# Spectral stage on Trainium2: transposed tiles hold neighbouring frequencies in pairs, with the input's and the tokens' order changed to suit

## Chip, cores and metric

One core of a Trainium2 chip runs the whole program: a spectral layer, a mixture of experts with top-1 routing and a feed-forward layer with maxima. The metric is the device time of one execution in microseconds. Matrix products that need accuracy are written as sums of a rounded part and a rest (`...h` and `...l`), so one product is three matmuls; matmuls of plain float32 operands appear as two instructions each.

## What is computed

```python
X = np.fft.rfft(x, axis=1)                     # x: 8 x 3072 x 256
Yr = Xr @ w_r - Xi @ w_i + b_r
Yi = Xr @ w_i + Xi @ w_r + b_i
Yr = np.sign(Yr) * np.maximum(np.abs(Yr) - 0.01, 0)     # Yi alike
y = np.fft.irfft(Yr + 1j * Yi, n=3072, axis=1)
x = y.reshape(8 * 3072, 256)
skip = (x @ w_skip) <= 0                       # such tokens pass through
e = argmax(x @ w_gate); x += gate * (relu(x @ w1[e]) @ w2[e])
h = np.maximum(np.maximum(x @ v1, x @ v2), x @ v3)
out = h @ w_out
```

## The kernel before

Three functions run one after the other: `spectral`, `experts`, `feed_forward`. Only `spectral` is changed. It treats the 8 batches in turn, and a transform of 3072 = 96 x 32 points is done in two steps of matmuls with a transposition of 32 x 32 blocks on VectorE between them.

*Forward.* `f1_mm` (L264) multiplies a chunk of the input, 96 partitions by 32 times 16 columns, by a 96-point transform; the result lies in a PSUM bank. `f1_tr` (L268) transposes the bank on VectorE into `g2`, a tile of 128 partitions, 32 frequencies and 256 channels; 24 of the 32 are used (`NF`), and the memory of the other eight, `spare(g2)`, later holds `y1s`. Sixteen groups `g` make up a batch. `f2` (L281) takes 128 channels of one frequency of `g2` as the weights (the stationary operand) and the matrix `c2` of that frequency as the moving one.

*Middle.* In a loop over 12 pairs of frequencies, `i`, TensorE runs `f2(i)`, then `wmm(i-1)` (the complex product with the weights, L316), then `if2(i-2)` (the first inverse step, L345). ScalarE and VectorE round and subtract between them (L132, L135, L288, L323 to L328), and ScalarE evicts the result of `if2` into two tiles `zs`, one for each half of the channels (L347).

*Inverse.* `z_tr` (L352) transposes a whole `zs` of 4096 elements per partition into `zt`. `if1` (L357) takes single frequencies of `zt` as weights, four of them in a bank, and ScalarE evicts the bank with a rearrangement (L358) into `y0` (first half) or `y1` (second half). `to_rows` (L364, L365) turns 128 tokens back into rows and adds the gate's scores; ScalarE puts them into `yk` (L366), and the SP queue stores 256 columns of them to DRAM (L367), 24 blocks of 128 tokens per batch. `gating` and `dispatch` (L461) later send the rows to their experts.

The schedule is the order of the code, on every engine. Behind the loop over `i` of a batch that has a successor stand: groups 0 to 3 of the next batch's `f1` (within the last turn), `f1` of groups 4 to 9, `z_tr` of the first half, `if1` for eight groups of it, `z_tr` of the second half, `f1_tr` of groups 4 to 9, `f1` and `f1_tr` of groups 10 to 15, and then for each of eight groups `if1` of the second half and `to_rows` of the group before. Since `y1s` is memory of the next `g2`, the first of those evictions waits until the last `f1_tr` is done. Meanwhile VectorE decodes weights of the feed-forward stage (`decode`, L475 to L527), up to two units per batch; it reads pairs of 32-bit words as `lo, hi = w[:, :, 0], w[:, :, 1]`, so at a step of two words. The last batch has no `f1` to do, and runs `gating` in pieces between the groups. PSUM tags A to D have two banks each, the inputs `xc` four buffers, and `z` tiles three.

Of the kernel before, what the change touches and what calls it, by code (L numbers as in the profile page):

```python
# [21 lines left out]
NF = 24  # L22
# [15 lines left out]
def _constants():  # L38
# [59 lines left out]
    tok = 32 * (32 * r[None] + p // 4) + 4 * g[None] + p % 4  # L98
# [69 lines left out]
def spectral(tc, ins, rows, xo, wsc, base, small, ident, split, feed, G):  # L168
    nc = tc.nc
    x = ins["x"]  # L170
    with ExitStack() as ctx, ExitStack() as early:
# [31 lines left out]
        def load_x(b, chunks):  # L203
            t = []
            for c in chunks:
                a = xp.tile([N1, N2, 32], F32, tag="x", name="xc")
                nc.sync.dma_start(out=a, in_=x[b, c])
                t.append(a)
            return t

        with tc.manual_schedule():
# [49 lines left out]
            def f1_mm(b, xt, g, tag):  # L261
                p = bank(tag, (N2, 16))
                c, o = divmod(g * 16, 32)
                nc.tensor.matmul(p, lhsT=f1, rhs=xt[c][:, :, o:o + 16])  # L264
                return p

            def f1_tr(g2, g, p):
                nc.vector.transpose(  # L268
                    out=g2[:, :, 16 * g:16 * g + 16].rearrange("p s d -> p d s"),
                    in_=p.rearrange("p n d -> p d n"),  # L270
                )

            def spare(g2):
                return g2[:, NF:32].rearrange("p s d -> p (s d)")

            def f2(g2, i, meanwhile=None):
                p = bank("B", (4, 128))
                for j in range(2):
                    f = 2 * i + j
                    for k in range(2):  # L280
                        nc.tensor.matmul(  # L281
                            p[:, 2 * j + k], lhsT=g2[:, f, 128 * k:128 * k + 128], rhs=c2[:, f]
                        )
# [53 lines left out]
            def if2(zs, i, y):  # L337
                p = bank("D", (2, 256))
                for j in range(2):
                    f = 2 * i + j  # L340
                    if i == NP - 1:
                        nc.tensor.matmul(p[:, j], lhsT=ic2[:, j], rhs=y[:, j])
                        continue
                    for n, (a, w) in enumerate(((ic2h, y[0]), (ic2l, y[0]), (ic2h, y[1]))):
                        nc.tensor.matmul(p[:, j], lhsT=a[:, f], rhs=w[:, j], start=(n == 0), stop=(n == 2))  # L345
                for h in range(2):
                    nc.scalar.activation(  # L347
                        out=zs[h][:, 2 * i:2 * i + 2], in_=p[:, :, 128 * h:128 * h + 128], func=AF.Copy
                    )

            def z_tr(zs, zt):
                nc.vector.transpose(out=zt.rearrange("p n e -> p e n"), in_=zs.rearrange("p f e -> p e f"))  # L352

            def if1(zt, dst, g):
                p = bank("D", (4, N1))
                for j in range(4):
                    nc.tensor.matmul(p[:, j], lhsT=zt[:, 4 * g + j], rhs=ic1)  # L357
                nc.scalar.activation(out=dst.rearrange("p (m n) -> p n m", n=4), in_=p, func=AF.Copy)  # L358

            def to_rows(b, g, y0, y1):  # L360
                for r in range(3):
                    t = 3 * g + r
                    p = bank("ABC"[r], (CW,))
                    nc.tensor.matmul(p[:, 0:CW // 2], lhsT=y0[:, 128 * r:128 * r + 128], rhs=gi[:, 0:CW // 2])  # L364
                    nc.tensor.matmul(p[:, CW // 2:CW], lhsT=y1[:, 128 * r:128 * r + 128], rhs=gi[:, CW // 2:CW])  # L365
# [3 lines left out]
                            "(m n) d -> m n d", n=N2  # L369
                        )[:, 4 * g:4 * g + 4],  # L370
# [178 lines left out]
            def new_g2():  # L549
                return ec.tile([128, 32, 256], F32, tag="g2", name="g2")  # L550
# [39 lines left out]
            for b in range(B):  # L590
# [11 lines left out]
                zs = [zp.tile([128, 32, 128], F32, tag="z", name=f"zs{h}") for h in range(2)]  # L602
                for t in zs:
                    nc.gpsimd.memset(t[:, NF:32], 0.0)
# [48 lines left out]
                def trans(h):  # L653
                    zt = zp.tile([128, 32, 128], F32, tag="z", name=f"zt{h}")
# [536 lines left out]
def _layout(name, a):  # L1191
    if name == "x":
        a = a.reshape(B, N1, N2, 8, 32).transpose(0, 3, 1, 2, 4)
# [32 lines left out]
```

## Time and profile before

| | |
|---|---|
| median of 3 runs | 3028.78 us (3018.82 to 3028.97) |
| the profiled execution | 3028.35 us, its span 3026.6 us |
| mean granted clock of TensorE | 0.979 |
| TensorE matmul / weight loads busy | 2891.4 us (96%) / 2502.2 us (83%) |
| VectorE / ScalarE / GpSimd busy | 1919.2 (63%) / 1407.6 (47%) / 1222.3 us (40%) |

PE is TensorE, PEld its weight loads (which overlap matmuls), DVE VectorE, ACT ScalarE, POOL GpSimd, SP the engine that issues most transfers. In the timelines a row is a group of like instructions that follow each other: start in us, time from the first start to the last end, what it is, and in brackets the idle time of the engine before it and what ended that. In the groups by line stand the number of instructions, their busy time in us and the mean in ns, then the idle time before them. In the stretches stand the length in us, the busy time and count of PE, PEld, DVE, ACT and POOL, then the granted clock, the transfers' share of 16 engines, and GB/s. A busy share says little of one stage: the spectral stage, up to some 893 us of the span, is read by itself.

### The profile page before, as it was taken

How to read it: one execution, taken by the hardware profiler on the slowest of the kernel's cores; microseconds unless marked ns; L12 is line 12 of the kernel's file. 1: busy time of each engine (PE TensorE's matmuls, PEld its weight loads, DVE VectorE, ACT ScalarE, POOL GpSimd, SP SyncE). 2: the span in 40 equal slices, each digit the busy share in tenths (PEclk: the TensorE clock that was granted, in tenths of full speed). 3: DMA queues.
4: the chain of work that ended last, by engine and by line, in shares of the span. 5: the costliest groups of instructions: out<-in, count | busy, mean ns of one | idle time of the engine just before them, and what ended most of it. 6: DMA issues, size and time to landing. Idle time of an engine off the chain costs nothing.

```text
span 3026.6 us, 53435 instructions
## 1 busy us (share of the span) xinstructions
PE 2891.4 (96%) x17158; PEld 2502.2 (83%) x17159; DVE 1919.2 (63%) x2707; ACT 1407.6 (47%) x2657; POOL 1222.3 (40%) x1206
## 2 busy tenths in 40 slices
PE   9989889999969999999789999999999999999998
PEld 7779878977959999999767777777777777777776
DVE  7887888778654544545365666666666666666664
ACT  4435544544532333333245555545555555545553
POOL 2032132223242222223245556555555556555554
PEclk9999999999979999999989999999999999999999
DMA  5323332331133333333355665566555665566543
GB/s 151 122 65 111 110 95 78 110 118 50 68 137 107 94 101 100 92 101 101 87 151 161 176 176 161 162 169 180 164 162 162 176 176 161 162 169 180 164 148 112
DMA packets 402461, 398.84 MB, mean 132 GB/s; under 512 B 274962, under 2 KB 320614, under 8 KB 402292
## 3 DMA queue, kind: packets, MB, share of 16 engines
q1 hardware_dynamic: 387732, 369.81, 43.3%
q0 software_dynamic: 14560, 26.86, 2.5%
q8 instruction: 97, 1.59, 0.2%
q14 instruction: 72, 0.59, 0.1%
HBM read 307.69 MB, written 101.91 MB: 135 GB/s over the span
## 4 chain that ended last, share of the span: by engine, by line
PE 45%; DVE 3%; ACT 1%; issue 1%; DMA 0%; SPq 0%; POOL 0%; DVEq 0%
PE pa L1040 18%; PE o_ps L1118 12%; PE pb L1040 10%; PE pc L1040 4%; DVE m L1086 1%; ACT hh L1097 1%; DVE xl L999 1%; DVE m L1050 0%; ACT xh L996 0%; DVE xc L978 0%; DMA xs<-xt 0%; SPq L972 0%; POOL hl L1098 0%; DVE xt L983 0%; DVE t L1050 0%
## 5 line engine op out<-in xcount | busy, mean ns | idle before, releaser
L1040 PE MATMUL pa<-xh,wu 128*128 128x512 f32 x1728 | 616.8, 397 | 19.5 <-ACT xh L996 19.2
L1047 ACT ACTIVATE s<-pa 128x512 f32<-128x512 f32 x648 | 378.6, 595 | 339.4 <-PE pa L1040 216.4
L1098 POOL TENSOR_TENSOR hl<-m,hh 128x512 fp32r<-128x512 f32 x288 | 398.0, 1403 | 301.4 <-ACT hh L1097 301.4
L1040 PEld LDWEIGHTS pa<-xh,wu 128*128 128x128 f32 x1728 | 326.1, 189 | 99.7 <-ACT xh L996 19.4
L1040 PE MATMUL pb<-xh,wu 128*128 128x512 f32 x864 | 348.3, 403 | 7.4 <-DVE m L1050 5.9
L1040 PE MATMUL pa<-xl,wu 128*128 128x512 f32 x864 | 343.2, 397 | 3.7 <-DVE xl L999 3.7
L1118 PE MATMUL o_ps<-hh,wo 128*128 128x512 f32 x1152 | 340.7, 398 | 3.4 <-ACT hh L1097 3.4
L1077 POOL TENSOR_TENSOR t<-s,s 128x512 f32<-128x512 f32 x144 | 186.5, 1295 | 268.4 <-ACT s L1047 268.4
L1118 PEld LDWEIGHTS o_ps<-hh,wo 128*128 128x128 f32 x1152 | 217.4, 189 | 57.1 <-ACT hh L1097 4.7
L907 ACT ACTIVATE hh<-h_ps 128x512 fp32r<-128x512 f32 x208 | 119.7, 597 | 298.1 <-PE h_ps L902 288.2
L1047 ACT ACTIVATE s<-pb 128x512 f32<-128x512 f32 x216 | 129.3, 599 | 272.3 <-PE pb L1040 272.0
L1086 DVE TENSOR_TENSOR m<-m,t 128x1536 f32<-128x1536 f32 x144 | 251.7, 1748 | 0.0
L908 DVE SCALAR_TENSOR_TENSOR hl<-h_ps,hh 128x512 fp32r<-128x512 f32 x208 | 138.7, 689 | 175.9 <-ACT hh L907 158.3
L925 PE MATMUL y_ps<-w2l,hh 128*128 128x256 f32 x832 | 236.1, 284 | 0.6 <-POOL w2l L770 0.2
L925 PE MATMUL y_ps<-w2h,hl 128*128 128x256 f32 x832 | 235.7, 283 | 0.1
L925 PE MATMUL y_ps<-w2h,hh 128*128 128x256 f32 x832 | 235.3, 283 | 0.0
L461 POOL DMA_INDIRECT rows<-yk,pos x192 | 195.2, 1017 | 92.8 <-issue 64.1
L902 PE MATMUL h_ps<-xh,w1h 128*128 128x256 f32 x832 | 230.1, 277 | 1.6 <-DVEq L884 1.6
L902 PE MATMUL h_ps<-xl,w1h 128*128 128x256 f32 x832 | 230.1, 277 | 0.0
L902 PE MATMUL h_ps<-xh,w1l 128*128 128x256 f32 x832 | 229.8, 276 | 0.0
L1040 PEld LDWEIGHTS pb<-xh,wu 128*128 128x128 f32 x864 | 163.1, 189 | 65.1 <-DVE m L1050 15.9
L1050 DVE TENSOR_TENSOR t<-pc,s 128x512 f32<-128x512 f32 x144 | 99.3, 689 | 167.3 <-PE pc L1040 137.1
(248 smaller groups left out, 7212.7 us busy)
## 6 DMA issues: line engine op xcount, KB each, us to landing
wu<-wsc SPq DMA_DIRECT2D x216, 896.0 KB
xc<-in_x_dram SPq DMA_DIRECT2D x64, 384.0 KB
xt<-yk SPq DMA_DIRECT2D x192, 128.0 KB
xs<-xt SPq DMA_DIRECT2D x192, 128.0 KB
out_dram<-ob SPq DMA_DIRECT2D x192, 128.0 KB
xr<-rows SPq DMA_DIRECT2D x53, 264.0 KB
xs<-rows SPq DMA_DIRECT2D x208, 64.0 KB, 2.3
w1f<-in_moe_w_dram SPq DMA_DIRECT2D x9, 1024.0 KB, 4.9
```

The source lines that it names most:

```text
L461: a = nc.gpsimd.indirect_dma_start(out=rows[:, :], out_offset=bass.IndirectOffsetOnAxis(ap=pos, axis=0), in_=yk[:, t, G:G + RW], in_offset ...
L902: nc.tensor.matmul(p[:, j], lhsT=a[:, k, f0:f0 + 128], rhs=v[:, k], start=(i == 0), stop=(i == 5))
L907: nc.scalar.activation(out=hh[:, sl], in_=p, func=AF.Relu)
L908: nc.vector.scalar_tensor_tensor(out=hl[:, sl], in0=p, scalar=0.0, in1=hh[:, sl].bitcast(F32), op0=ALU.max, op1=ALU.subtract)
L925: nc.tensor.matmul(y, lhsT=a[:, c, 128 * j:128 * j + 128], rhs=v[:, c], start=(i == 0), stop=(i == 23))
L1040: nc.tensor.matmul(o, lhsT=self.w[:, g, at:at + 128], rhs=v[h], start=(start and i == 0), stop=(i == 2), skip_group_check=True,)
L1047: nc.scalar.activation(out=self.s[k], in_=o, func=AF.Copy)
L1050: nc.vector.tensor_tensor(out=self.t[:, i], in0=o, in1=self.s[k], op=ALU.add)
L1077: nc.gpsimd.tensor_tensor(out=self.t[:, 2], in0=self.s[5], in1=self.s[7], op=ALU.add)
L1086: nc.vector.tensor_tensor(out=m[:, 0:3], in0=m[:, 0:3], in1=self.t, op=ALU.max)
L1098: nc.gpsimd.tensor_tensor(out=hl[:, i], in0=m[:, i], in1=hh[:, i].bitcast(F32), op=ALU.subtract)
L1118: nc.tensor.matmul(o, lhsT=wo[g][:, 2 * p + c, 128 * k:128 * k + 128], rhs=h[v][:, (0, 3, 1, 2)[2 * t + c]], start=(p == 0 and i == 0), st ...
```

## The change

The two tiles that VectorE's transposes write or read, `g2` and `zs`/`zt`, are laid out with two neighbouring frequencies (or, in `zt`, two neighbouring positions) next to each other: from `[128, 32, n]` to `[128, 16, n, 2]`. Everything that touches them follows:

- the transposes of `f1_tr` and `z_tr` name the pair as their innermost dimension, on both sides;
- the input `x` is laid out on the host with 32 channels ahead of 32 positions, so the bank of `f1_mm` holds the positions of a channel next to each other, and the moving operand of `f1_mm` is one run of 512 words (before: runs of 16);
- the weights of `f2` and of `if1` are now every second word of a row of 256;
- ScalarE's eviction of `if2` writes every second word of `zs`;
- ScalarE's eviction of `if1` writes runs of 32 words (before: every fourth word), which puts the tokens of a block in another order: partition `p` holds the token `32 * (32 * r + p % 32) + 4 * g + p // 32`. The table `c_tok`, which tells the dispatch each row's token, and the DRAM side of the store follow; the store's DRAM side has the dimensions 4 x 32 x 256 instead of 32 x 4 x 256.

The number of instructions on each engine, their order and their sizes stay.

```diff
-    tok = 32 * (32 * r[None] + p // 4) + 4 * g[None] + p % 4
+    tok = 32 * (32 * r[None] + p % 32) + 4 * g[None] + p // 32
...
-                a = xp.tile([N1, N2, 32], F32, tag="x", name="xc")
+                a = xp.tile([N1, 32, N2], F32, tag="x", name="xc")
...
-                p = bank(tag, (N2, 16))
+                p = bank(tag, (16, N2))
                 c, o = divmod(g * 16, 32)
-                nc.tensor.matmul(p, lhsT=f1, rhs=xt[c][:, :, o:o + 16])
+                nc.tensor.matmul(p, lhsT=f1, rhs=xt[c][:, o:o + 16])
...
                 nc.vector.transpose(
-                    out=g2[:, :, 16 * g:16 * g + 16].rearrange("p s d -> p d s"),
-                    in_=p.rearrange("p n d -> p d n"),
+                    out=g2[:, :, 16 * g:16 * g + 16].rearrange("p s d t -> p d s t"),
+                    in_=p.rearrange("p d (s t) -> p d s t", t=2),
                 )
...
-                return g2[:, NF:32].rearrange("p s d -> p (s d)")
+                return g2[:, NF // 2:16].rearrange("p s d t -> p (s d t)")
...
-                            p[:, 2 * j + k], lhsT=g2[:, f, 128 * k:128 * k + 128], rhs=c2[:, f]
+                            p[:, 2 * j + k], lhsT=g2[:, i, 128 * k:128 * k + 128, j], rhs=c2[:, f]
...
-                        out=zs[h][:, 2 * i:2 * i + 2], in_=p[:, :, 128 * h:128 * h + 128], func=AF.Copy
+                        out=zs[h][:, i].rearrange("p e j -> p j e"), in_=p[:, :, 128 * h:128 * h + 128], func=AF.Copy
...
             def z_tr(zs, zt):
-                nc.vector.transpose(out=zt.rearrange("p n e -> p e n"), in_=zs.rearrange("p f e -> p e f"))
+                nc.vector.transpose(
+                    out=zt.rearrange("p n e t -> p e n t"), in_=zs.rearrange("p f e t -> p e f t")
+                )
...
-                    nc.tensor.matmul(p[:, j], lhsT=zt[:, 4 * g + j], rhs=ic1)
-                nc.scalar.activation(out=dst.rearrange("p (m n) -> p n m", n=4), in_=p, func=AF.Copy)
+                    nc.tensor.matmul(p[:, j], lhsT=zt[:, 2 * g + j // 2, :, j % 2], rhs=ic1)
+                nc.scalar.activation(
+                    out=dst.rearrange("p (r n m) -> p n r m", r=3, n=4),
+                    in_=p.rearrange("p n (r m) -> p n r m", r=3), func=AF.Copy,
+                )
...
                         out=xo[b * S + 1024 * r:b * S + 1024 * r + 1024].rearrange(
-                            "(m n) d -> m n d", n=N2
-                        )[:, 4 * g:4 * g + 4],
+                            "(m n) d -> n m d", n=N2
+                        )[4 * g:4 * g + 4],
                         in_=yk[:, t, G:G + D],
...
-                return ec.tile([128, 32, 256], F32, tag="g2", name="g2")
+                return ec.tile([128, 16, 256, 2], F32, tag="g2", name="g2")
...
-        a = a.reshape(B, N1, N2, 8, 32).transpose(0, 3, 1, 2, 4)
+        a = a.reshape(B, N1, N2, 8, 32).transpose(0, 3, 1, 4, 2)
```

## Rows read from the trace of the kernel before

**Rows 1.** Busy time in stretches: engines, granted clock, transfers.

```profile
24.90:893.00 868.10, 792.40 (x5810) 722.77 (x5810) 667.21 (x1042) 426.96 (x934) 233.21 (x305) 0.96 0.30 97
296.45:329.00 32.55, 24.14 (x117) 17.22 (x115) 31.31 (x23) 9.35 (x14) 11.75 (x16) 0.90 0.24 74
329.00:354.00 25.00, 24.99 (x200) 24.79 (x201) 17.59 (x41) 18.38 (x42) 1.17 (x2) 0.93 0.57 198
```

**Rows 2.** Groups by line, 0 to 1700 us: two TensorE groups that wait.

```profile
L357 PE MATMUL bankD<-ic,zt 128*128 128x96 f32 x1024 | 150.1, 306 | 41.6 <-DVE zt L352 34.3 <-issue 5.0 <-ACT y L358 1.0
L365 PE MATMUL bankA<-gi,g 128*128 128x137 f32 x112 | 23.8, 295 | 18.6 <-ACT g L358 18.6
```

**Rows 3.** Timeline of TensorE, behind the main loop of batch 2.

```profile
301.19 1.88 PE L264 MATMUL bankC<-xc,f 96*128 96x512 f32 x4
307.83 10.45 PE L357 MATMUL bankD<-ic,zt 128*128 128x96 f32 x64 [4.76 <-DVE zt L352]
318.12 1.91 PE L264 MATMUL bankA<-xc,f 96*128 96x512 f32 x4
...
323.30 1.92 PE L357 MATMUL bankD<-ic,zt 128*128 128x96 f32 x16
325.06 0.42 PE L364 MATMUL bankA<-gi,y 128*128 128x137 f32 x2
328.96 0.50 PE L365 MATMUL bankA<-gi,g 128*128 128x137 f32 x2 [3.48 <-ACT g L358]
```

**Rows 4.** Timeline of VectorE there: the transposes, first and last.

```profile
296.45 1.95 DVE L268 STREAM_TRANSPOSE g<-bankA 128x512 f32<-128x512 f32 x2
...
299.99 16.04 DVE L352 STREAM_TRANSPOSE zt<-zs 128x4096 f32<-128x4096 f32 x2
...
326.10 1.85 DVE L268 STREAM_TRANSPOSE g<-bankC 128x512 f32<-128x512 f32 x2
```

**Rows 5.** Groups by line, 0 to 1700 us: transposes and evictions.

```profile
L352 DVE STREAM_TRANSPOSE zt<-zs 128x4096 f32<-128x4096 f32 x16 | 129.6, 8101 | 2.8 <-ACT zs L347 1.8
L347 ACT ACTIVATE zs<-bankD 128x256 f32<-128x256 f32 x192 | 63.2, 381 | 178.7 <-PE bankD L345 174.2 <-PE bankD L342 3.0 <-DMA wsc<-dec 1.4
L358 ACT ACTIVATE y<-bankD 128x384 f32<-128x384 f32 x64 | 56.6, 885 | 116.4 <-PE bankD L357 94.9 <-issue 12.9 <-PE bankA L264 5.1
L268 DVE STREAM_TRANSPOSE g<-bankA 128x512 f32<-128x512 f32 x46 | 45.3, 1060 | 8.3 <-PE bankA L264 5.6 <-PE bankC L264 2.1 <-PE bankB L264 0.5
L1047 ACT ACTIVATE s<-pa 128x512 f32<-128x512 f32 x77 | 45.0, 595 | 39.5 <-PE pa L1040 25.6 <-DVE m L1085 12.9
L785 DVE STREAM_TRANSPOSE xt<-xs 128x512 f32<-128x512 f32 x52 | 37.0, 711 | 18.6 <-DMA xs<-rows 17.9
```

**Rows 6.** The same view: the decode's reads of adjacent and of every second word.

```profile
L476 DVE TENSOR_SCALAR dec<-dec 128x512 int32<-128x512 int32 x12 | 5.1, 427 | 0.4
L479 DVE TENSOR_SCALAR dec<-dec 128x512 int32<-128x512 int32 x12 | 5.0, 420 | 0.0
```

**Rows 7.** The same view: weight loads of if1 and f2.

```profile
L357 PEld LDWEIGHTS bankD<-ic,zt 128*128 128x128 f32 x1024 | 143.4, 220 | 54.2 <-issue 49.2 <-ACT y L358 3.6 <-ACT dec L358 0.6
L281 PEld LDWEIGHTS bankB<-c,g 128*128 128x128 f32 x768 | 93.4, 191 | 3.1 <-DVE xl L135 1.5 <-DVE g L268 1.4 <-issue 0.2
```

**Rows 8.** Timeline of TensorE, the last batch's first if1.

```profile
841.28 7.54 PE L357 MATMUL bankD<-ic,zt 128*128 128x96 f32 x48 [4.29 <-DVE zt L352]
```

**Rows 9.** Timelines of TensorE and VectorE, main loop of batch 2.

```profile
281.02 1.05 PE L281 MATMUL bankB<-c,g 128*128 128x128 f32 x8
...
285.00 0.29 PE L345 MATMUL bankD<-yl,ic2h 128*128 128x256 f32 x1
...
283.77 0.69 DVE L135 TENSOR_TENSOR yl<-v,yh 128x512 fp32r<-128x512 f32 x1 [0.28 <-ACT yh L132]
```

**Rows 10.** Timeline of the SP queue in batch 2, and transfers by issue.

```profile
332.34 0.37 SPq L517 DMA_DIRECT2D dec<-in_moe_w_out_dram  x1
...
xt<-yk SPq DMA_DIRECT2D x192, 128.0 KB
```

More of the change, by code (lines that the diff above doesn't have):

```diff
@@ L363, in to_rows @@
                     p = bank("ABC"[r], (CW,))
-                    nc.tensor.matmul(p[:, 0:CW // 2], lhsT=y0[:, 128 * r:128 * r + 128], rhs=gi[:, 0:CW // 2])
-                    nc.tensor.matmul(p[:, CW // 2:CW], lhsT=y1[:, 128 * r:128 * r + 128], rhs=gi[:, CW // 2:CW])
+                    for y, o in ((y0, 0), (y1, CW // 2)):
+                        nc.tensor.matmul(
+                            p[:, o:o + CW // 2], lhsT=y[:, 128 * r:128 * r + 128],
+                            rhs=gi[:, o:o + CW // 2],
+                        )
                     nc.scalar.activation(out=yk[:, t], in_=p, func=AF.Copy)
@@ L601, in spectral @@
                     g2n = None
-                zs = [zp.tile([128, 32, 128], F32, tag="z", name=f"zs{h}") for h in range(2)]
+                zs = [zp.tile([128, 16, 128, 2], F32, tag="z", name=f"zs{h}") for h in range(2)]
                 for t in zs:
-                    nc.gpsimd.memset(t[:, NF:32], 0.0)
+                    nc.gpsimd.memset(t[:, NF // 2:16], 0.0)
                 ys = {}
@@ L653, in trans @@
                 def trans(h):
-                    zt = zp.tile([128, 32, 128], F32, tag="z", name=f"zt{h}")
+                    zt = zp.tile([128, 16, 128, 2], F32, tag="z", name=f"zt{h}")
                     z_tr(zs[h], zt)
```

## The prediction

> **What bounds the kernel now.** I read the busy time by stretches first. In the spectral stage, 24.9 to 893 us, TensorE is busy 792 of 868 us and VectorE 667, and the mean granted clock is 0.96 [rows 1]. So the stage holds some 76 us in which TensorE does nothing, and the question is who ends them. The idle times ahead of TensorE's groups name it: 34.3 us until `zt` (VectorE's large transpose, L352) plus 5.0 us of the same wait in the first batch, put down to "issue", and 18.6 us until ScalarE's `g` (L358) [rows 2]. The last wait is VectorE's too: ScalarE's eviction writes into the spare part of `g2`, so it has to wait for the last small transpose (L268).
>
> The timeline of batch 2 shows where this happens. TensorE finishes three groups of `f1` matmuls at 303.07, stands still for 4.76 us until the first large transpose is done, runs 64 `if1` matmuls in 10.29 us, 12 `f1` matmuls in 5.18, 16 `if1` matmuls in 1.76, and waits again for 3.48 us, until 328.96 [rows 3]. VectorE meanwhile has no gap worth naming: 16 small transposes and two large ones from 296.45 to 327.95 [rows 4], which is 31.31 busy of 32.55 us [rows 1]. In this stretch, once in each of the seven batches that have a successor, VectorE's transposes set the time. Before it, in the main loop, TensorE is dense and VectorE has slack; behind it, in 329 to 354, TensorE is busy 24.99 of 25.00 us [rows 1].
>
> **The change part by part.** *Transposes.* A small one (512 elements, steps of 16 words in and 256 words out) takes 1060 ns, and the one over 4096 elements 8101; the nearest transpose that reads and writes runs of 32 words or more takes 711 for 512 [rows 5]. Now elements come in adjacent pairs, on the read side (`z_tr`) or the write side (both). No row shows a pair that hops, so the price lies between those two. I take the lower, for this reason: VectorE's decode reads every second word (L479) in 420 ns, and an operation of the same kind on adjacent words (L476) in 427 [rows 6], so a step of 8 bytes costs nothing, while ScalarE's write at a step of 16 bytes (L358) takes 885 ns for 384 elements, where 512 and 256 adjacent ones take 595 and 381, hence 488 for 384 [rows 5]. Something between 8 and 16 bytes doubles the cost, and two adjacent words at a landing stay on the cheap side of it. Back to back a transpose costs some 0.165 us less than its duration (two take 1.95, so 0.89 from start to start [rows 4, 5]), so a small one comes to 0.54 us, and a large one to 711 - 165 = 546 ns per 512, eight times that: 4.4 us, 4.5 with its start.
>
> [...]
>
> *ScalarE.* The 128 evictions of L358 now write runs of 32 words: 488 instead of 885 ns. The 192 evictions to `zs` (L347, 381 ns) now write at a step of 8 bytes: between 381 (as the reads on VectorE) and 381 + 256 x 1.03 = 645 (the surcharge per element of L358). I take 381. At 645, two of them would delay the `yh` of the same turn by up to 0.5 us; `yl` is ready at 284.46 and its matmul starts at 285.00 [rows 9], so that is nearly covered. Uncovered it would cost up to 0.3 us in each of about 90 turns, 26 us, and I keep that for the upper end.
>
> *Weights of `f2` and `if1`.* 768 and 1024 weight loads [rows 7] now read at a step of 8 bytes. No row shows a strided weight load. Below: no cost, as on VectorE; above: twice, as the transposes and L358 show for larger hops. I take none, by the nearer row (8 bytes). The rival below has the other end.
>
> *The rest.* The `x` loads carry the same bytes in rows of 4 KB, and the matmuls of `f1` read adjacent words instead of runs of 16: I keep their rate. The memsets, constants and dispatches keep sizes and places; each engine's order of instructions stays. The 192 stores of `yk` have the same bytes, rearranged (third rival).
>
> *Sum for batch 2.* Four small transposes from 296.45 end at 298.6; the large one can follow if ScalarE has filled `zs` (it has by 299.99 at the latest [rows 4]; waiting that long would cost 1.4 us a batch), and ends at 303.1. TensorE comes from `f1` at 303.07: the wait of 4.76 goes, but for some 0.1 to 0.3. The 64 `if1` matmuls were slow to start and then held by evictions; now they run at the 0.110 us of the later 16 [rows 3]: 7.0 instead of 10.29. They end at 310.2. The 12 `f1` matmuls (5.2) need banks that VectorE has emptied: second large transpose done at 307.5, six small ones by 310.8, in step. TensorE reaches 315.4, then the 16 `if1` (1.76): 317.1, then 0.25 until the matmul that stood at 328.96. VectorE's last transpose ends by 316.2 and the eviction by 316.9, so the 3.48 goes as well. Gain 328.96 - 317.4 = 11.6 us.
>
> Over the seven batches: 35.0 of waits for `zt` (34.3 + 5.0 less the last batch's 4.29 [rows 2, 8]) + 18.6 + 7 x 3.3 = 76.7, less 1.5 that is left of the first wait: 75. [...] As not every batch need pay it I take 0.7 each: 5. The last batch has nothing beside the large transposes: its `if1` waits 4.29 us until 841.28 [rows 8] for one, and the second sets the next step; two times 3.6 = 7, and 1 from faster evictions: 8. The 16 small transposes ahead of the first batch I leave at nothing, since loads run beside them; a microsecond there is part of the low end. Sum **88**.
>
> Behind the gap nothing is due earlier than it can come: stretch 329 to 354 is TensorE's own and only moves. VectorE's decode moves with it.
>
> **The rivals.** *(A) The pair helps only in part*, by 1.5 ns per element instead of 1.05: large transposes 6.2, small ones 0.75. Then 2 x 6.2 + 16 x 0.75 = 24.4 from 296.45, 320.9, and 321.5 behind the eviction: gain 7.5 per batch. With the last batch some 58 us; 2970. The same range holds a weight load a fifth slower (1792 x 22 ns = 39 us lost).
>
> *(B) The pair helps nothing*: VectorE's 31.4 us stay, only evictions gain 0.4 per batch and a little in the last: about 5 us, 3023. For it: the hop behind a pair is as long as before. Against: rows 6.
>
> *(C) The strided weight load is slow*, and the kernel is slower. Loads and matmuls of `if1` follow each other at 0.110 us [rows 3] and those of `f2` about as fast, eight in 1.05 us with the end of the last [rows 9], with nothing beside them; if the load takes double, each of the 1792 adds 0.110: 197 us lost against 88 won, 3028 + 109 = 3137. It decides from 88 / 1792 = 49 ns per load on. For it: loads are as dense as the matmuls, 191 to 220 ns each [rows 7], so nothing hides them. Against: the 8-byte read of rows 6. [...]
>
> *(D) The stores run on fewer transfer queues*: their DRAM side had 32 as its outermost count, now 4. Stretch 329 to 354 moves 198 GB/s x 25 = 4.95 MB at a share of 0.57 [rows 1], of which 24 x 128 KB [rows 10] = 3.1 MB are stores: 0.64 x 0.57 x 16 x 25 = 145 queue-us per batch; on four queues 36 us each, where the stretch has 25. Some 11 us then run on into the next batch, whose `x` is needed 60 us later. Only the second decode's load (332.34 [rows 10], behind three stores, 4.5 us) could come up to 2 us late, in five batches: 10 us at most, 2950. [...]
>
> **How the numbers follow.** The profiled execution took 3028.35 us around a span of 3026.6, 0.4 below the median shown, so no correction: 3028.35 - 88 = 2940. Chances: forecast 0.68, (A) 0.12, (D) 0.06, (B) 0.05, (C) 0.09. The low end is a gain of 105: the clock's 1.7 in all batches (7 more), and `f1`, the start and the last batch 10 better together. The high end takes in (A) and (D); (B) and (C), 0.14, are left out. A measurement here can tell about 0.5%, 15 us, from no change. Faster 0.86 (forecast, A, D), same 0.05 (B), slower 0.09 (C).
>
> **What would show it.** Right: L352 near 4.5 us and L268 near 0.7; the waits for `zt` and `g` at L357 and L365 nearly gone; the 64 `if1` in about 7 us; L358 near 490 ns; PEld of L281 and L357 still about 190; L347 near 381. Wrong: L352 over 6 us, weight loads over 240 ns, more than 0.2 us of wait per turn for `yl`, or `dec` waiting for its load.

## The result, and the profile after

The changed kernel takes 2977.51 us (median of 4 runs, 2972.22 to 2978.88), the kernel before 3027.24 beside it: a ratio of 0.984, 95% interval 0.9828 to 0.9852. The gain is 49.7 us where 88 were forecast, and 2977.51 lies above 2970, the time of rival (A), which the range was drawn to take in. The profiled execution was the fastest of the four, 2972.22 us; it has a span of 2970.5 us and a mean clock of 0.987, and its gain on the profiled execution of before (span 3026.6) is 56.1 us. Line numbers behind the diff are up to 8 higher (L357 is now L359, L358 L360, L364 and L365 both L370, L366 L374, L367 L375, L510 and L544, the decode's load and store, L518 and L552).

Groups by line of the changed kernel, 0 to 1700 us:

```profile
L352 DVE STREAM_TRANSPOSE zt<-zs 128x4096 f32<-128x4096 f32 x16 | 70.8, 4427 | 2.8 <-ACT zs L347 1.8
L268 DVE STREAM_TRANSPOSE g<-bankA 128x512 f32<-128x512 f32 x46 | 30.9, 696 | 19.3 <-PE bankA L264 12.9 <-PE bankB L264 6.0
...
L359 PE MATMUL bankD<-ic,zt 128*128 128x96 f32 x1024 | 130.1, 280 | 3.3 <-DVE zt L352 2.9 <-PE bankC L264 0.3
L370 PE MATMUL bankA<-gi,g 128*128 128x137 f32 x112 | 22.9, 285 | 3.1 <-ACT g L360 3.1
L316 PE MATMUL bankC<-wih,x 128*128 128x256 f32 x32 | 9.8, 325 | 10.5 <-DVE x L300 10.5
...
L359 PEld LDWEIGHTS bankD<-ic,zt 128*128 128x128 f32 x1024 | 126.2, 196 | 13.1 <-PE bankC L264 8.1 <-issue 5.0
L281 PEld LDWEIGHTS bankB<-c,g 128*128 128x128 f32 x768 | 98.5, 197 | 3.6 <-DVE xl L135 2.3 <-DVE g L268 0.8 <-issue 0.5
...
L347 ACT ACTIVATE zs<-bankD 128x256 f32<-128x256 f32 x192 | 66.2, 405 | 179.1 <-PE bankD L345 176.1 <-PE bankD L342 2.8 <-issue 0.2
L360 ACT ACTIVATE y<-bankD 128x384 f32<-128x384 f32 x64 | 31.5, 492 | 82.1 <-PE bankD L359 61.5 <-PE bankA L264 10.5 <-issue 10.1
```

The prices of the transposes and of the eviction came as taken: 4427 and 696 ns, 492 ns [rows 5]. The waits for `zt` and `g`, 34.3 and 18.6 us [rows 2], are 2.9 and 3.1. What is new stands in the row of L316: TensorE waits 10.5 us until VectorE's `x` (the tile `x0`, which the first `f2` of the next batch prepares). VectorE's own row says why, and SP's timeline in batch 2 says what goes on there. The group row and a timeline row of VectorE come first, then SP's timeline (a row's length is the time from the first issue to the end of the last), all of the changed kernel:

```profile
L298 DVE CAST x<-xh 128x256 fp32r<-128x256 f32 x8 | 2.3, 290 | 14.4 <-DMA wsc<-dw 14.4
...
324.70 0.29 DVE L298 CAST x<-xh 128x256 fp32r<-128x256 f32 x1 [3.28 <-DMA wsc<-dw]
```

```profile
304.62 1.71 SPq L375 DMA_DIRECT2D xt<-yk  x3
308.16 0.38 SPq L525 DMA_DIRECT2D dec<-in_moe_w_out_dram  x1
308.63 6.48 SPq L375 DMA_DIRECT2D xt<-yk  x6
315.20 3.77 SPq L552 DMA_DIRECT2D wsc<-dw  x4
319.06 20.06 SPq L375 DMA_DIRECT2D xt<-yk  x15
```

`x0` has the buffer tag `yl`, and so has the last quarter of the first decode's result, `dw`. Its four transfers `wsc<-dw` stand in SP's queue behind nine stores. The first three stores take SP 0.57 us each; then six take 1.08 and fifteen 1.34, while blocks become ready every 0.78 us. The store has become the slower of the two, and what stands behind it comes late. In batch 2 TensorE pays twice, as its timeline shows:

```profile
325.40 0.39 PE L316 MATMUL bankC<-wih,x 128*128 128x256 f32 x1 [2.35 <-DVE x L300]
...
326.22 0.41 PE L316 MATMUL bankC<-wih,x 128*128 128x256 f32 x1
...
329.21 0.41 PE L316 MATMUL bankC<-wih,xl 128*128 128x256 f32 x1
```

It waits 2.35 us first. Then, from 326.22 to 329.21, come 14 steps of 0.214 us instead of 0.118, which is 1.35 us more; the granted clock is 0.50 there, and 1.00 from 320 to 324 us. This second payment is not made in every batch: of the five batches that wait for `x0`, three fall to 0.50 (from 223.9 to 227.2, 326.22 to 329.21 and 428.7 to 431.8 us, behind waits of 1.83, 2.35 and 2.63 us) and two do not (behind 1.03 and 2.13). The stretches (columns as in [rows 1]) show the clock in the first, third and fifth of these batches, 1.00, 0.66 and 1.00, and in batch 2 transfers at 0.39 and 0.48 of the 16 engines just when stores pile up:

```profile
123.00:128.00 5.00, 4.12 (x35) 4.12 (x36) 4.46 (x13) 2.12 (x5) 0.00 (x0) 1.00 0.27 96
325.00:330.00 5.00, 4.60 (x26) 4.60 (x27) 2.83 (x9) 0.42 (x1) 0.00 (x0) 0.66 0.28 93
528.00:533.00 5.00, 3.98 (x33) 3.98 (x34) 3.94 (x12) 0.70 (x3) 0.00 (x0) 1.00 0.26 83
...
303.00:328.00 25.00, 22.14 (x178) 21.60 (x177) 17.76 (x40) 16.74 (x41) 1.43 (x2) 0.96 0.39 123
328.00:354.00 26.00, 26.00 (x214) 26.00 (x214) 19.42 (x42) 12.66 (x30) 0.18 (x1) 0.97 0.48 142
```

So in batch 2 the gap (the stretch behind the main loop) was shortened by 10.0 us (11.6 forecast), and some 3 were given back before the next gap.

### The profile page after: what moved, and what is told of

It reads as the page before. It is cut to its first block, busy times and chain, and to the rows that moved or that the text cites. A ratio compares the mean times of both kernels' runs of the same rounds, so it can differ in the third digit from the quotient of the medians.

```text
span 2970.5 us, 53442 instructions
## 1 busy us (share of the span) xinstructions
PE 2876.5 (97%) x17158; PEld 2492.8 (84%) x17159; DVE 1835.7 (62%) x2707; ACT 1374.1 (46%) x2657; POOL 1224.4 (41%) x1206
## 3 DMA queue, kind: packets, MB, share of 16 engines
q1 hardware_dynamic: 385428, 369.80, 44.4%
## 4 chain that ended last, share of the span: by engine, by line
PE 45%; DVE 3%; ACT 1%; issue 1%; DMA 0%; SPq 0%; POOL 0%; DVEq 0%
PE pa L1048 19%; PE o_ps L1126 12%; PE pb L1048 10%; PE pc L1048 5%; DVE m L1094 2%; ACT hh L1105 1%; DVE xl L1007 1%; DVE m L1058 0%; ACT xh L1004 0%; DVE xc L986 0%; DMA xs<-xt 0%; SPq L980 0%; POOL hl L1106 0%; DVE xt L991 0%; DVE t L1058 0%
## 5 line engine op out<-in xcount | busy, mean ns | idle before, releaser
L1105 ACT ACTIVATE hh<-m 128x512 fp32r<-128x512 f32 x288 | 165.7, 626 | 81.4 <-DVE m L1094 81.4
```

Of the source, the lines that this page charges most:

```text
L1105: nc.scalar.activation(out=hh[:, i], in_=m[:, i], func=AF.Copy)
```

## The experiments

The runs were on several chips, where the kernel before took between 3012 and 3027 us; across these the ratios to the kernel before are compared. Runs of one set share a chip and its runs of the kernel before; the sets are e1 to e4, e5 to e8, e9 and e10, e11 and e12, e13 and e14, e15 to e17.

### First group: which part

**e1**: the change with the old token order and store; the eviction now makes its hop (a step to an element that is not the next in memory) where it reads.

```diff
-    tok = 32 * (32 * r[None] + p % 32) + 4 * g[None] + p // 32
+    tok = 32 * (32 * r[None] + p // 4) + 4 * g[None] + p % 4
...
-                    out=dst.rearrange("p (r n m) -> p n r m", r=3, n=4),
-                    in_=p.rearrange("p n (r m) -> p n r m", r=3), func=AF.Copy,
+                    out=dst.rearrange("p (m n) -> p m n", n=4), in_=p.rearrange("p n m -> p m n"), func=AF.Copy,
...
-                            "(m n) d -> n m d", n=N2
-                        )[4 * g:4 * g + 4],
+                            "(m n) d -> m n d", n=N2
+                        )[:, 4 * g:4 * g + 4],
```

> The pairs stay; token order and store are those of before (DRAM side's outermost count 32), and ScalarE's eviction writes adjacent words and reads PSUM at a step of 96 words instead. Theory S (the stores): with an outermost count of 4 a store of `yk` runs on four transfer queues, the stores back up, `wsc<-dw` comes late behind them, `x0` of the next batch waits for it, and TensorE for `x0`, after which its clock is low for some 3 us; about 18 us in six batches. Then here the wait of L298 for `wsc<-dw` (14.4 us) and TensorE's wait for `x0` (10.5 us) are gone, 15 stores take about 0.8 us each at SP instead of 1.34, and the time is 2960 us (2955 to 2966). Rival W (the strided weight loads and the first wait are the whole miss, the stores hidden): 2977 us, within 4. If the read of PSUM at a step costs what the write at a step of 16 bytes did (885 ns instead of 490), up to 10 us come on top of either.

Measured: 2958.72 us, ratio 0.9774 (0.9757 to 0.979). As theory S has it. Groups by line, 0 to 1700 us, and SP's timeline in batch 2:

```profile
L298 DVE CAST x<-xh 128x256 fp32r<-128x256 f32 x8 | 2.3, 282 | 0.0
...
L316 PE MATMUL bankC<-wih,x 128*128 128x256 f32 x32 | 8.4, 285 | 0.5 <-DVE x L300 0.5
...
L360 ACT ACTIVATE y<-bankD 128x384 f32<-128x384 f32 x64 | 31.4, 491 | 82.8 <-PE bankD L359 63.2 <-PE bankA L264 10.4 <-issue 9.2
```

```profile
303.62 3.80 SPq L374 DMA_DIRECT2D xt<-yk  x6
307.51 2.03 SPq L551 DMA_DIRECT2D wsc<-dw  x4
309.64 10.99 SPq L374 DMA_DIRECT2D xt<-yk  x15
```

The wait for `wsc<-dw` is gone, fifteen stores take 10.99 us, and the eviction costs 491 ns with a read of PSUM at a step of 96 words. Against the change, whose kernel before had the same 3027 us, that is 18.8 us between the medians. Between the profiled executions it is 13.8 (spans of 2970.5 and 2956.7), and all of it comes in the first five batches, the ones with a second decode, which are 14.7 us shorter together: their distance from one first `if1` to the next is 97.2 to 98.5 us here and 99.0 to 102.1 in the change; in the other two, 98.2 and 96.5 against 98.2 and 96.1. Where the other 5 us of the medians lie no trace shows, since the change's other three executions took 2976.70 to 2978.88 us and only the fastest has a trace.

**e2**: the same with the old eviction (`out=dst.rearrange("p (m n) -> p n m", n=4), in_=p`).

> Only the transposed tiles and the layout of the input are changed; token order, eviction and store are those of before. Theory S: no wait for `x0`, so 2960 us, plus the dearer evictions (885 ns): at most 2.7 us in each of seven batches for 64 `if1` matmuls (10.29 us before, 7.60 now) and 0.5 per batch at the end of the gap, so 2964 to 2983. Rival W: the same surcharge on 2977, so 2981 to 3000. The wait of L298 for `wsc<-dw` decides without the sum: gone by S, 14 us by W (there it hides).

Measured: 2964.88 us, ratio 0.9792. L298 does not wait for `wsc<-dw`; theory S. The dear eviction (880 ns) costs 6 us against e1.

**e3**: the kernel before with the change's token order, eviction and store alone.

> The kernel before with the new token order, eviction and store alone, no pairs. Theory S: the store's price shows here too: some 18 us lost for late `wsc<-dw`, while the eviction (490 instead of 885 ns) gains 0.4 us at the end of each batch's gap and up to 2.7 in the 64 `if1` matmuls: 3.5 to 22 us; so 3023 to 3042. Rival W: 3005 to 3024. SP's issue of 15 stores goes from 0.77 to about 1.3 us each by S.

Measured: 3037.46 us, ratio 1.0036 (1.0026 to 1.0046). The new store alone makes the old kernel slower by 10 us, although the eviction takes 490 ns; L298 waits 7.1 us for `wsc<-dw`.

**e4**: the change with four stores of 32 rows per block (`for j in range(4)`: `[4 * g + j]` from `yk[32 * j:32 * j + 32, t, G:G + D]`).

> The change with every store of `yk` cut in four of 32 rows each, so that each has an outermost count of 32; the rows in DRAM, their order and the eviction stay. Theory S with the count of queues as cause: 2960 us (2955 to 2968; 96 issues per batch instead of 24 could cost SP some of it). Rival O (it is the order in which the rows go to DRAM, 32 KB apart, that slows them, not the number of queues): 2977 us, within 4, and SP's stores stay at 1.3 us for 128 KB. Rival W: 2977 too, but with the waits of L298 gone or not without effect.

Measured: 3003.17 us, ratio 0.992; none of the three. In SP's timeline of batch 2, 60 stores of 32 KB take 30.06 us, 0.50 each, so an issue costs SP some 0.5 us even for a quarter of the bytes, and 96 of them make `wsc<-dw` later still (L298 waits 29.0 us). It says nothing of queues; e15 to e17 do.

### Second group: the wait, and the weight loads

**e5**: e1 with weight loads of 128 adjacent words.

```diff
-lhsT=zt[:, 2 * g + j // 2, :, j % 2]
+lhsT=zt[:, 2 * g + j // 2].rearrange("p e t -> p (e t)")[:, 128 * (j % 2):128 * (j % 2) + 128]
```

(and `f2` alike)

> As e1, but the weight loads of `f2` and `if1` read 128 adjacent words of the same 256 instead of every second one; the values are then others, so the routing and the expert stages after it differ, and what counts is when the experts' first matmul of w1 starts (841.15 us in e1), and the pace before it. Theory W (a load at a step of 8 bytes is slower by some 6 to 10 ns where loads follow each other): 64 `if1` matmuls start within 7.0 us instead of 7.60, PEld of L359 and L281 are at 190 to 192 ns instead of 196, a turn of the main loop takes 4.44 instead of 4.49, and the experts start 10 to 14 us earlier, at 827 to 831. Rival V (the slower pace comes from ScalarE's `zs` write at 405 instead of 381 ns and from later semaphores): nothing changes, 840 to 842.

Measured: the experts start at 831.94 us (841.15 in e1), 1 us later than forecast. This run's first `if1` came 1.85 us later than e1's, because TensorE was slow twice in the first 31 us (its first four `f1` instructions take 3.75 us, 1.96 in e1, and from 27.06 to 30.50 us its matmuls come every 0.214 us, the pace of the granted clock of 0.50 in the change); the stage from there on took 742.8 instead of 753.9: 11 us. (The whole time, 2962.55, holds other routing.) Theory W, though not with all of the 11 us. From the first `if1` to that of the last batch it is 676.2 us, against 684.2 in e1 and 683.3 in e13, the same kernel again: 7 to 8. The rest lies in the last batch, whose gating works on other values here and whose length differs even between runs of one kernel (e11 and e14 below). Groups of weight loads, 0 to 1700 us, and two turns of the main loop (passes of the loop over `i`) on TensorE, of e5:

```profile
L359 PEld LDWEIGHTS bankD<-ic,zt 128*128 128x128 f32 x1024 | 120.4, 191 | 14.3 <-PE bankC L264 8.2 <-issue 5.9 <-ACT yk L373 0.2
L281 PEld LDWEIGHTS bankB<-c,g 128*128 128x128 f32 x768 | 93.4, 191 | 2.3 <-DVE xl L135 1.5 <-issue 0.5 <-DVE g L268 0.3
...
319.18 1.05 PE L281 MATMUL bankB<-c,g 128*128 128x128 f32 x8
...
323.63 1.05 PE L281 MATMUL bankB<-c,g 128*128 128x128 f32 x8
```

and the same turns of e1:

```profile
324.85 1.10 PE L281 MATMUL bankB<-c,g 128*128 128x128 f32 x8
...
329.35 1.10 PE L281 MATMUL bankB<-c,g 128*128 128x128 f32 x8
```

4.45 us a turn against 4.50, 191 against 196 ns a load [rows 7]. The `zs` write at 405 ns is in both, so it is not that. 64 `if1` matmuls start within 7.26 us against 7.60; the 7.0 of the forecast did not come even with adjacent words.

**e6**: `wsc<-dw` of the first decode issued by ScalarE (`(nc.sync if last else nc.scalar).dma_start(...)`).

> The change with one edit: the four transfers `wsc<-dw` of the first decode are issued by ScalarE, whose transfer ring is another than SP's; the stores of `yk` stay on an outermost count of 4. Theory S (dw waits in line behind the stores of its own ring): the wait of L298 for `wsc<-dw` falls from 14.4 us to under 4, TensorE's for `x0` from 10.5 to under 3, and the time is 2962 us (2957 to 2968; ScalarE pays some us for the issues). Rival E (the transfer engines that carry the stores are full, in which ring dw stands does not matter): over 10 us of wait remain and the time is 2974 to 2980. Rival P (SP itself is late in issuing, 1.34 us per store): the same as S for dw, but the waits for the second decode's load stay, 5 us or less.

Measured: 2996.95 us, ratio 0.9906. The wait of L298 for `wsc<-dw` is gone altogether and TensorE's for `x0` is 0.5 us, as S and P have it; but the time rose. ScalarE's timeline in batch 2 and a TensorE group (0 to 1700 us) of e6:

```profile
326.34 2.97 ACTq L552 DMA_DIRECT2D wsc<-dw  x2
329.36 0.49 ACT L360 ACTIVATE g<-bankD 128x384 f32<-128x384 f32 x1 [4.71 <-DMA wsc<-dw]
...
L370 PE MATMUL bankA<-gi,g 128*128 128x137 f32 x112 | 26.1, 317 | 29.7 <-ACT g L360 29.7
```

While ScalarE issues two transfers, for 2.97 us, it evicts nothing, and TensorE waits for `g` 29.7 us instead of 3.1. The cause is confirmed, the remedy is none.

**e7**: the halves of `dw` swap buffers (`(("yh", "yl"), ("v", "c"))`).

> The change with one edit: the two halves of the first decode's result swap their buffers, so that the one that `x0` reuses (`yl`) is carried off by the second of the four transfers `wsc<-dw` and not by the last; `v` is then the last, and is next written one turn later. Theory S: `x0` comes two transfers earlier, about 1.9 us in each of five batches where its wait is 2.6 to 3.3: 4 to 6 us of the 14.4 remain, the time is 2968 us (2965 to 2972), and no wait of like size appears at `v` (L325). Rival X (the wait for `x0` is covered by something else that ends as late, the second decode's load or a store's ring): the wait of L298 shrinks but the time stays at 2975 to 2980.

Measured: 2963.39 us, ratio 0.9791 (0.9775 to 0.9807). VectorE's L298, 0 to 1700 us:

```profile
L298 DVE CAST x<-xh 128x256 fp32r<-128x256 f32 x8 | 2.3, 289 | 8.2 <-DMA wsc<-dw 7.4 <-ACT yk L374 0.8
```

TensorE waits 4.4 us for `x0` instead of 10.5. The wait of L298 is half of the change's 14.4 and longer than the 4 to 6 that theory S gave; the time is below its range. By the ratios, swapping two names wins back about 15 of the 19 us; by the traces (from the first `if1` to the last batch's, 690.9 us here, 698.5 in the change, 684.2 in e1) 7.6 of 14.3. The store is unchanged, so what is won back was not the store's own time but that of what waits behind it.

**e8**: two stores of 64 rows per block with an outermost count of 16, the tokens in pairs (`tok = 32 * (32 * r + 2 * (p // 8) + p % 2) + 4 * g + p // 2 % 4`).

> Two stores per block, of 64 rows each with an outermost count of 16; the tokens of a block stand in pairs, and ScalarE's eviction writes two adjacent words at a hop. e4's four stores cost SP about 0.5 us each whatever their size, which made SP late; here two cost 1.0 us per block against the 0.78 in which a block is finished, so SP is late by 1.4 us when `wsc<-dw` is due. Theory K (the number of queues was the cause in the change, and SP's issues in e4): L298 waits 4 to 9 us in all and the time is 2963 to 2971, if evictions take between 490 and 885 ns. Rival O (the order of the rows in DRAM): the stores back up as in the change, 14 us of wait or more, and 2977 or more.

Measured: 2959.71 us, ratio 0.9783; L298 waits 2.1 us for `wsc<-dw`, evictions take 529 ns. Theory K, a little better than its range.

### Third group: which side of the transpose

**e9** keeps pairs only where a transpose reads (`zt` is `[128, 32, 128]` again, `g2` too), **e10** only where it writes.

> As e1, but only what the transposes read stands in pairs or adjacent (`xt`, PSUM, `zs`); what they write (`g2`, `zt`) is laid out as before, so each of the 32 words of a write lands alone, 256 or 128 words apart, and weight loads read adjacent words. Theory R (the hop on the read side was the price): L352 near 4.4 us, L268 near 0.69, and as weight loads are adjacent too (e5: 11 us) the time is 2947 us (2942 to 2953). Theory L (the hop at the landing was the price, as with ScalarE's write, while its read of PSUM at a step of 96 words cost nothing in e1): L352 stays at 8.1 us and L268 near 1.06, the waits for `zt` and `g` are back, and the time is 3000 to 3020. Theory H (either side costs its part): L352 5.5 to 7, 2960 to 2990.

> As e1, but only what the transposes write (`g2`, `zt`) stands in pairs; `xt`, PSUM and `zs` are laid out as before, so each word is read alone, 16 or 128 words from the last, and ScalarE writes `zs` adjacent (L347 back from 405 to 381 ns). Weight loads stay at a step of 8 bytes. Theory L (landing): L352 near 4.4 us, L268 near 0.69, 2957 us (2953 to 2961). Theory R (reading): L352 8.1 us, L268 1.06, 3005 to 3025. Theory H: L352 5.5 to 7, 2970 to 3000.

Measured: ratio 0.9937 (0.9921 to 0.9954; 2994.09 us) and 0.9896 (0.9879 to 0.9912; 2980.54 us). Groups by line, 0 to 1700 us, of e9 and then of e10:

```profile
L352 DVE STREAM_TRANSPOSE zt<-zs 128x4096 f32<-128x4096 f32 x16 | 115.4, 7210 | 2.8 <-ACT zs L347 1.8
L268 DVE STREAM_TRANSPOSE g<-bankA 128x512 f32<-128x512 f32 x46 | 44.6, 1041 | 6.1 <-PE bankA L264 6.1
```

```profile
L352 DVE STREAM_TRANSPOSE zt<-zs 128x4096 f32<-128x4096 f32 x16 | 115.9, 7244 | 2.8 <-ACT zs L347 1.8
L268 DVE STREAM_TRANSPOSE g<-bankA 128x512 f32<-128x512 f32 x46 | 30.7, 694 | 9.2 <-PE bankA L264 8.2
```

The large transpose, SBUF to SBUF, needs the pairs on both sides: either side alone leaves 7.2 of 8.1 us, which none of the theories had. The small one reads PSUM, and there only the landing counts, as theory L has it: 1041 without, 694 with pairs at it.

**e11** is e1 with the old input layout, **e12** e1 with pairs in `zs` and `zt` alone.

> As e1, but the input keeps its old layout, so `f1` reads runs of 16 words and the small transposes read PSUM at a step of 16 words; everything else stands in pairs. By e10, where L268 took 692 ns with that read, a step in PSUM costs a transpose nothing: L268 at 0.69 us, L352 at 4.43, and the ratio to the kernel before is that of e1, 0.9774 within 0.002 (2959 us where the kernel before takes 3027). Rival: part of e1's gain comes from adjacent reads by `f1` or the `x` rows of 4 KB; then 3 to 10 us more, a ratio of 0.9785 to 0.981.

> As e1, but `g2` is laid out as before, so the small transposes land word by word (by e9 1.03 us, 0.87 from start to start, instead of 0.54) and `f2` reads its weights adjacent; `zs` and `zt` stay in pairs. VectorE then has 4 x 0.87 + 9.0 + 12 x 0.87 = 22.9 us in the gap, where TensorE's own work with its short waits takes 23.3 in e1; the first `if1` starts 1.3 us later, and the last eviction 1 to 1.5 later. Theory G (the pairs in `g2` are worth little, since VectorE no longer sets the end): 7 x 1.3 = 9 us lost, 5 won by 768 adjacent weight loads at 6 ns each: a ratio of 0.979 (0.977 to 0.981). Rival Z (VectorE sets the end again, since each small transpose comes only when its bank is full): 3 us lost in each of seven batches, 16 net, 0.981 to 0.985.

Measured: e11 0.9757 (0.9739 to 0.9774; 2940.99 us), e12 0.9799 (0.9781 to 0.9817; 2953.6 us). The new layout of the input gains nothing; L268 is at 695 ns without it. The pairs in `g2` are worth about 0.004: they save the wait for `zt` (9.7 us in e12) and cost the dearer loads of `f2` (a turn takes 4.45 us in e12). e11 and e1 differed in one more thing, VectorE's last transposes in a gap, of e1 and then of e11:

```profile
292.30 0.72 DVE L268 STREAM_TRANSPOSE g<-bankA 128x512 f32<-128x512 f32 x1 [1.33 <-PE bankA L264]
293.70 0.72 DVE L268 STREAM_TRANSPOSE g<-bankA 128x512 f32<-128x512 f32 x1 [0.68 <-PE bankB L264]
```

```profile
290.83 1.58 DVE L268 STREAM_TRANSPOSE g<-bankA 128x512 f32<-128x512 f32 x2 [0.67 <-PE bankA L264]
```

In e1 they come every 1.4 us, though the `f1` matmuls they wait for start every 0.86, and TensorE has its `g` 8.1 us after the first of these (7.3 in e11). **e13** and **e14** put the two kernels on one chip.

> The kernel of e1 once more, now beside that of e11 on one chip. In e1, in six of its seven gaps, VectorE's last six transposes waited for the `f1` matmuls 1.42 us each instead of 0.86, and TensorE met `g` 8.1 us after the start of those matmuls; in e11 it was 7.3 in all seven. Theory C (that belongs to the chip the run was on: the gaps of the kernel before show such waits on its chip as well, and e12 with the new input layout, on e11's chip, shows none): both kernels of this call show the same, all 7.3 or all about 8.0, and their times agree within 3 us. Theory I (the new input layout makes `f1` slow while GpSimd dispatches): this one 8.0 in six gaps, e11's kernel 7.3, and 5 to 7 us between them.

> The kernel of e11 once more, on the chip of e13. Theory C: the same as e13 within 3 us. Theory I: 5 to 7 us less than e13.

Measured: 2957.06 us, 0.9772 (0.9759 to 0.9786), and 2956.16, 0.9774 (0.9761 to 0.9788); 7.9 to 8.0 us in six gaps of both. So it does not come from the input's layout. That it comes from the chip is not shown: e11 and e14 are one kernel, both are on record with chip number 15, and the median is 2940.99 us in one and 2956.16 in the other. Of the 13.8 us between their spans (2939.5 and 2953.3) the seven batches up to the last one's first `if1` hold 4.9 and the last batch 11.0 (57.7 us from there to the experts in e11, 68.7 in e14), and the later stages give 2 back. In that last batch of e14 VectorE's gating waits up to 5.6 us for something that the profile does not name; in e11 it never does. Why such waits end late in some runs and not in others is open; in the one gap with nothing to dispatch, the first, no run shows it.

### Fourth group: the count of queues or the order of rows

**e15 to e17**: e1 with its store cut at group 16, 25 or 17 of its 32 groups of four rows; rows, bytes and number of stores are the same in all three. The edit against e1, of e17:

```diff
-                    nc.sync.dma_start(
+                    for lo, hi in ((0, 17), (17, 32)):
+                        nc.sync.dma_start(
...
-                        )[:, 4 * g:4 * g + 4],
-                        in_=yk[:, t, G:G + D],
...
+                            )[lo:hi, 4 * g:4 * g + 4],
+                            in_=yk[4 * lo:4 * hi, t, G:G + D],
```

> As e1 (token order, rows and eviction of before), but every store of `yk` is cut in two, 16 and 16 of its 32 groups of four rows. The rows go to DRAM as in e1; only the count of stores doubles. Control for the next two: L298 waits for `wsc<-dw` 1 to 4 us in all, as in e8, a ratio to the kernel before of 0.977 to 0.980.

> As e15, cut 25 and 7. Theory K (a store uses as many queues as its outermost count can be divided into equal parts by, 16 at most): 5 and 7 queues, the fullest gets 24 KB per block; by the change's own pace (32 KB on each of four queues per 1.34 us) that is 1.0 us per block, just what two issues cost SP anyway, so a ratio of 0.977 to 0.982. Theory O (the number of queues is not the cause, but that the change writes single rows 32 KB apart instead of four adjacent ones): as e15.

> As e15, cut 17 and 15: the same rows, bytes and number of stores, one group of four rows moved from the second store to the first. Theory K: 17 is prime, so 68 KB of each block go through one queue, 2.9 us per block at the change's pace, where a block is made in 0.78; `wsc<-dw` behind nine blocks comes 15 us or more too late in each of five batches, L298 waits 60 us or more in all, and the kernel is near or above the time of before, a ratio of 1.00 to 1.03. Theory O: as e15, within 0.003.

Measured: 0.9777 (0.976 to 0.9793; 2957.79 us), 0.9861 (0.9844 to 0.9877; 2982.78 us) and 1.0291 (1.0274 to 1.0308; 3112.82 us). VectorE's L298 (0 to 1700 us) in e15, e16 and e17:

```profile
L298 DVE CAST x<-xh 128x256 fp32r<-128x256 f32 x8 | 2.3, 289 | 3.7 <-ACT yk L373 2.4 <-DMA wsc<-dw 1.3
```

```profile
L298 DVE CAST x<-xh 128x256 fp32r<-128x256 f32 x8 | 2.3, 290 | 18.2 <-DMA wsc<-dw 18.2
```

```profile
L298 DVE CAST x<-xh 128x256 fp32r<-128x256 f32 x8 | 2.3, 290 | 67.9 <-DMA wsc<-dw 67.9
```

One group of four rows moved from one store to the other costs 155 us. So it is the count, not the order of rows. The profile shows the count itself. These are SP's queue in the kernel before, the change, e15, e16 and e17 (packets, MB, share of 16 engines):

```profile
q1 hardware_dynamic: 387732, 369.81, 43.3%
q1 hardware_dynamic: 385428, 369.80, 44.4%
q1 hardware_dynamic: 390804, 369.82, 43.4%
q1 hardware_dynamic: 386964, 369.80, 43.4%
q1 hardware_dynamic: 387732, 369.81, 41.6%
```

The bytes are the same to 0.02 MB, so the packets that come and go are small ones. The change has 2304 fewer than the kernel before, 12 for each of its 192 stores. A second store per block adds 16 per block (before to e15); from e15 to e16 20 per block are gone, from e15 to e17 16. One small packet for each queue that a store runs on, with the queues that theory K gives, fits all of it: 16 before, 4 in the change, 16 + 16, 5 + 7 and 1 + 15. From 330 to 338 us of the change, where SP issues nothing but stores, 23 of 775 packets are under 512 bytes while 0.77 MB are moved, some six blocks: four for each. The transfers' share there is 0.27 of the 16 engines, some 4.4 of them. That e16, with at most 24 KB of a block on one queue by theory K, is worse than the change with 32 was not foreseen. SP's timelines in batch 2 show where it loses: from the first store to the first issue of `wsc<-dw` SP takes 7.9 us in e1, 10.6 in the change, 12.9 in e15, 15.3 in e16 and 26.9 in e17, and from the last issue of `wsc<-dw` to the first work on `x0` it is 7.0 us in the change, 2.5 in e15 and 4.2 in e16. So e16 is late at SP, where its two stores per block take 0.81 us each; why they take that long stays open.

## Why the prediction was wrong

**Right.** The bound (VectorE's transposes in the gap) and the direction. The price of a pair: 4.43 and 0.70 us against 4.4 to 4.5 and 0.7, though the step in bytes does not decide it: e1's eviction reads PSUM at a step of 96 words in 491 ns, and pairs at the landing alone leave the large transpose at 7.24 us (e10); L358 at 490; the waits gone; TensorE waits 0.4 us in all for `yl`, so the write of `zs` at a step of 8 bytes (405 ns, 381 taken) is covered. Rivals (A) and (B) fell with the first two rows, (C) with 196 ns: a load became dearer by about 6 ns, not by 49.

**The step that failed** is rival (D), and with it the sentence that behind the gap nothing is due earlier than it can come. (D) saw four queues and 36 us of stores and asked who waits behind them, but named two transfers only: the next `x`, 60 us away, and the second decode's load (for which VectorE waited 1.24 us in batch 2). It left out `wsc<-dw`, in the same queue behind nine stores, and the tile that waits for its buffer. SP's timeline before, of which [rows 10] has one row, shows it between the stores:

```profile
333.72 4.50 SPq L367 DMA_DIRECT2D xt<-yk  x6
338.31 2.03 SPq L544 DMA_DIRECT2D wsc<-dw  x4
340.43 11.56 SPq L367 DMA_DIRECT2D xt<-yk  x15
```

(D) also had the chance of a side case, 0.06, though e17 shows 155 us for the count of queues that it starts from. Its sum for the stores themselves was near: 36 us for 24 stores are 1.5 us each, and fifteen took 1.34. Its price, "10 us at most", was 14.3 us between the profiled executions (698.5 us from the first `if1` to the last batch's, 684.2 in e1) and 18.8 between the medians. The trace accounts for the 14.3: TensorE waits 10.0 us longer for `x0` (10.5 against 0.5), and three times it loses some 1.4 us at the granted clock of 0.50.

**Mis-sized.** "I take none" for strided weight loads: 7 to 8 us up to the last batch (e5), by steps (0.05 per turn, 0.04 per group of `to_rows`, 0.34 per 64 `if1`) some 10 over all eight batches. "Two times 3.6" in the last batch: both steps came, but not to the end. The first matmul of `to_rows` there, before and after:

```profile
852.80 0.43 PE L364 MATMUL bankA<-gi,y 128*128 128x137 f32 x2
794.89 0.43 PE L370 MATMUL bankA<-gi,y 128*128 128x137 f32 x2
```

VectorE's first large transpose starts at 833.03 and 781.67, so these come 19.77 and 13.22 us behind it, 6.55 us sooner. From there to the experts' first matmul it is 59.2 us before and 61.2 after, so 4.5 of the forecast 8 are left. In that stretch VectorE's gating has waits that the profile gives no cause for, of up to 6.1 us before and 7.9 after; whether they took the rest is open. "They end ... in step": in this run TensorE meets `g` 0.6 to 0.7 us later than in the first gap in each of the other six, some 4 us; in e11 no gap shows it. The 5 us for the clock (0.7 in each of seven batches) no run shows as a term: in batch 2 the granted clock of the gap and of the stretch behind it was 0.90 and 0.93 before [rows 1], 1.00 and 0.96 in the change (281 to 303 and 303 to 328 us), and 1.00 and 1.00 in e1 (276.5 to 300 and 298 to 323).

The profiled executions miss 31.9 of the 88 us, and 14.3 + 8 + 4 + 3.5 are 30 of them; the terms were measured in different runs and may share a microsecond or two. The medians miss 6 more, for which there is no trace. No one of the four would have put the time above 2970; their sum did.

**The versions.** e1 (0.9774; again 0.9772 as e13) and e14 (0.9774) beat both kernels; their intervals don't tell them apart, and e14 needs no new input layout. Against the change (0.984) they are some 20 us faster.

## What to carry to other kernels

A new layout that pays on one engine can be paid for by a transfer that touches it, as here by the store with an outermost count of 4 instead of 32 (14.3 us from the first `if1` to the last batch's, 698.5 against 684.2 in e1): look at the outermost count of each store, and go through its queue's order with the question which buffers are freed by what stands behind it. Where a hop can't be avoided, put it where it costs nothing: here the read of PSUM, by ScalarE (491 ns at a step of 96 words, e1) and by VectorE (694 ns at 16, e10), and not the landing in SBUF (885 in the kernel before and 1041 in e9).

## What the hardware showed beyond expectation

- With pairs of adjacent words on both sides the transpose of 4096 elements, SBUF to SBUF, takes 4427 ns instead of 8101, near the 4.4 us worked out from a transpose on longer runs (711 ns for 512 [rows 5]); with pairs on one side alone it takes 7210 (e9) or 7244 (e10), which saves 0.9 of 3.7 us.
- Weight loads at a step of 8 bytes take 196 ns (e1) instead of 191 (e5), and a dense row of eight `f2` matmuls 1.10 us instead of 1.05.
- A store's issue takes SP 0.50 us at 32 KB (e4) and 0.57 at 128 KB for the first three of batch 2 in the change; the last fifteen there, at an outermost count of 4, take 1.34 each (0.73 in e1, at 32), and on ScalarE two issues held evictions for 2.97 us (e6).
- The same kernel shows waits in one run that it lacks in another (e11 and e14: 7.3 and 7.9 to 8.0 us in six gaps, 57.7 and 68.7 us in the last batch, 15 us in all), so what is compared to a per cent has to run beside its kernel before.
- SP's queue has 12 packets fewer per store where the outermost count is 4 instead of 32 (385428 against 387732 over 192 stores), and one small packet for each queue of a store fits its counts in five kernels.
